# First scores from a quarter of each query block, the query rest of batch 0 in its own buffer, and the last highway pass in 128-column chunks

## The chip, the cores and the metric

The kernel runs on one core of one Trainium2 chip. The metric is the device time of one execution in microseconds (us), lower is better. Several runs are timed and their median is used; one execution more is recorded by the hardware profiler. The engines are called TensorE (PE in the profile, its weight loads PEld), VectorE (DVE), ScalarE (ACT), GpSimd (POOL) and SyncE (SP, which here only issues loads and stores).

## The reference: what is computed

Attention in which each query keeps only its 32 best keys, followed by a highway layer over the tokens:

```
q, k, v: 8 batches x 8 heads x 576 positions x 64, float32
scores = q @ k^T / 8
kth    = the 32nd largest score of each row
attn   = softmax of the scores >= kth, the others left out
y      = attn @ v                     # then heads side by side: x, 4608 x 512
H = relu(x @ w_h);  T = sigmoid(x @ w_t + b_t)
out = T * H + (1 - T) * x             # w_h, w_t: 512 x 512
```

## The kernel before

**Tiling.** The 576 positions of a batch are four chunks of 128 (J = 4) and a rest of 64 (R). Row `p` of the 128 partitions holds positions 4p to 4p+3, so query tile `qt` is made of the positions 4p + qt: one row in four. A *group* is one query tile of one batch; the rest rows of two batches together make a *joint* group. The order of the groups is that of the list `groups`; the very last one is called final and is `gl`, the one before it `gp`. A group of 128 rows has eight tiles, one for each head, taken two at a time: a *pair*, numbered n over the whole program, 0 to 143. The four pairs of group 0 use the heads 0-1, 2-3, 4-5, 6-7 and only the queries of row 0 in four, but all the keys.

**Loads and turning.** `load` (L105) brings two heads of q or k (`qin`, `kin`, 256 KB in two transfers) into SBUF; `load_rest` (L116) brings the 64 rest rows of all heads (`krest`, `qrest`, 128 KB each), `load_values` (L123) the values (1 MB) and their rest. TensorE turns each load into the layout that the scores need (`turn`, L138, four 128 x 128 transposes into one PSUM bank; `turn_rest`, L157), and ScalarE, or VectorE where `vec` is set, copies the bank into `kq`. The `kin` and `qin` pools have three buffers each, the rest tiles one. A bank for turning is one of two called `zt` or the only one called `fp`, which the highway layer uses too.

**One pair.** `scores` (L186) writes the scores of two tiles into the PSUM tile `ps`, of which there is one; `evac` (L206) has ScalarE copy it (with Relu) into a z buffer, `sc`; `tree` (L217) has VectorE take the larger of the left half, from `ps`, and the right half, from `sc`, into `hi`. So `ps` is free for the next scores only when both ScalarE and VectorE have read it. For each two pairs `folds` (L232) halves `hi` again, `minima` (L252) lets GpSimd work out the smaller halves, and `tops` and `rest` (L280, L301) find the 32nd largest with VectorE's eight-at-a-time maximum and replace. `mask` (L376) turns scores below the threshold into a penalty on ScalarE; `parts` (L425) transposes scores and penalty on TensorE and takes the exponential on ScalarE (`et`); `av` multiplies with the values and copies the result to `xs`, with the sum of the weights as a 65th column.

**The highway layer of a group.** `norm` (L490) divides by that sum; `ffn_x`, `ffn_h`, `ffn_r`, `ffn_d`, `ffn_t`, `ffn_e`, `ffn_o` (L588 to L685) turn x, make `h`, subtract half of x, make the tanh form of T, combine, and store. They are spread over the following steps.

**Order.** Every instruction on TensorE, VectorE, ScalarE and GpSimd keeps its written order (`Pinned`, L25), and so do the transfers issued through `ops.nc.queue`; other transfers on SP may be placed by the scheduler. Each engine runs its own list in order and waits at the head of it. A transfer on SP or ScalarE also waits until the transfer eight before it has landed, since there are eight semaphores for them. The loop at L892 takes one pair a step: tree of n, mask and values of earlier pairs, scores of n + 1, then the lists on VectorE. Before it, L832 to L856 load and turn the first data by hand. The loads of batch 1 begin at step 1 (`begin`, L802), and its turns use the `fp` bank at the end of steps from 4 on.

**The end.** From L979 the last three pairs (m, m + 1, m + 2) and the highway passes of `gp` and `gl` are written out by hand. There the final pass begins when both `values(m + 1)` and `values(m + 2)` are done: `norm(gl)`, `final_x(gl)`, then h, t, and the output in two halves. `judge_lists`, `judge_scales` and `judge` (L865 to L880) reduce range checks to one flag; if it is set, an exact and slower path follows (L1027), which these inputs do not take. All engines load the flag and branch on it at the end.

In the profile, instructions of the pinned engines all carry the line L35 of the `Pinned` helper, so they are told apart by the names of their tiles.

Of the kernel before, what the change touches and what calls it, by code (L numbers as in the profile page):

```python
# [8 lines left out]
AF = mybir.ActivationFunctionType  # L9
# [10 lines left out]
J = 4  # L20
# [47 lines left out]
class Ops:  # L68
# [36 lines left out]
    def load(self, pr, name, hp, eng=None, other=None):  # L105
# [4 lines left out]
        for hh in range(2):  # L110
            (other if other and hh else eng).dma_start(
                t[:, :, hh, :], src[hh].rearrange("(p j) d -> p j d", j=J)
            )
        pr[name, hp] = t

    def load_rest(self, pr, name, eng=None):  # L116
        t = self.ldpool.tile([self.R, self.H, self.D], FP32, tag=name, name=name, bufs=1)
        (eng or self.nc.sync).dma_start(
            t[:], pr[name[0]](0, self.H, J * self.P, self.S).rearrange("h p d -> p h d")
        )  # L120
        pr[name] = t
# [16 lines left out]
    def turn(self, pr, name, hp, bank=None, vec=False):  # L138
# [6 lines left out]
        for c in range(J):  # L145
# [5 lines left out]
        dst = pr["kq"][:, "kq".index(name[0]), hp, 0 : J * P]  # L151
        if vec:
            nc.vector.tensor_copy(dst, kqps[:])
        else:
            nc.scalar.copy(dst, kqps[:])

    def turn_rest(self, pr, h0, h1):  # L157
# [5 lines left out]
        for i, name in enumerate(("krest", "qrest")):  # L163
# [7 lines left out]
            pr["kq"][:, :, h0:h1, J * self.P : self.S], view[:, :, h0:h1, :]  # L171
        )

    def values_rest(self, pr):
        self.nc.scalar.copy(
            pr["vb"][0 : self.R, :, J, 0 : self.D], pr["vrest"][:]
# [40 lines left out]
    def tree(self, n):  # L217
# [3 lines left out]
        if n % 2 == 0:  # L221
# [5 lines left out]
        ps = self.st[n].pop("ps")  # L227
        nc.vector.tensor_tensor(
            hi[:, half, :], ps[:, :, 0:H1], self.st[n]["sc"][:, :, H1:S], ALU.max
# [271 lines left out]
    def norm_x(self, g):  # L501
# [8 lines left out]
        for hs in (slice(0, H // 2), slice(H // 2, H)) if g.final else (slice(0, H),):  # L510
            made = (nc.vector if g.final else nc.gpsimd).tensor_tensor(
                x3[:, hs, :],
                xs3[:, hs, 0:D],
                rinv[0:ql, hs].unsqueeze(2).to_broadcast([ql, hs.stop - hs.start, D]),
                ALU.mult,
            )
# [6 lines left out]
    def final_x(self, g):  # L523


        nc, P, n_g = self.nc, self.P, self.n_g
        g.xT = self.fpool.tile([P, n_g, P], BF16, tag="xT", name="xT")
        g.xh = self.fpool.tile([P, self.dm], FP32, tag="xh", name="xh")
        half = n_g // 2
        for i0 in (0, half):  # L530
            xtps = self.ztps.tile([P, 512], FP32, tag="zt", name="xtps")
# [569 lines left out]
```

## Time and profile before

| what | us |
|---|---|
| median of 3 runs (lowest to highest) | 874.24 (872.53 to 874.45) |
| the profiled execution, its own time | 874.66 |
| its span, first to last instruction | 872.9 |
| VectorE busy | 843.6 (97%) |
| first work of VectorE, a copy of turned queries | 7.22 |
| tree of pair 0, 1, 2, 3 starts | 10.56, 14.55, 19.02, 23.05 |
| last list operation of VectorE ends | 854.45 |
| last copy to `xs` ends | 861.18 |
| last output operation of VectorE ends | 868.23 |

The span is shorter than the execution's own time by what lies before the first and after the last instruction. Rows of a timeline give a start, a length, the engine, the tile written and the tiles read; what stands in brackets is how long the engine sat idle before it and what ended that. A wait is put down to the last thing that came. Granted clock is the share of full speed at which TensorE was allowed to run.

### The profile page before, as it was taken

The page shows a single profiled execution, that of the slowest core. Times are in us where ns is not written, and L with a number is a line of the kernel's source. Part 1 is how long each engine was busy: PE and PEld are TensorE (multiplying, and loading weights), DVE is VectorE, ACT ScalarE, POOL GpSimd, SP SyncE. Part 2 cuts the span into 40 slices and gives each one's busy share as a digit, 9 for nine tenths or more (in the row PEclk, how much of TensorE's full clock was granted, in tenths as well). Part 3 has the DMA queues.
Part 4 walks back from the last instruction along what each step waited for, and adds up shares of the span by engine and source line. Part 5 has one row for each costly group of instructions (what it writes and reads, how often), then busy time and mean ns, then how long its engine had stood idle before and what let it go on. Part 6 is the DMA issues. An engine that isn't in the chain of part 4 may idle for free.

```text
span 872.9 us, 19884 instructions
## 1 busy us (share of the span) xinstructions
PE 707.8 (81%) x6569; PEld 500.4 (57%) x6569; DVE 843.6 (97%) x4200; ACT 695.9 (80%) x1244; POOL 690.8 (79%) x447
## 2 busy tenths in 40 slices
PE   6777988879788788778788798887978878887975
PEld 5455655655565555655565565665556655555653
DVE  4999999999999999999999999999999999999995
ACT  3788878888788887888888887888878888677784
POOL 5788887888878888888888888878888888877880
PEclk9799999999999998999999999999989999899898
DMA  9553422234234331323323432323412111111111
GB/s 196 130 110 62 109 38 57 60 62 98 37 62 92 73 86 29 70 67 62 86 50 56 96 80 56 62 64 69 105 37 46 42 37 38 37 26 25 26 39 38
DMA packets 104494, 57.06 MB, mean 65 GB/s; under 512 B 82112, under 2 KB 91712, under 8 KB 104384
## 3 DMA queue, kind: packets, MB, share of 16 engines
q1 hardware_dynamic: 92768, 37.37, 17.0%
q0 software_dynamic: 10416, 17.96, 13.6%
q8 instruction: 53, 0.87, 0.4%
q14 instruction: 57, 0.47, 0.2%
q10 hardware_dynamic: 1200, 0.39, 0.2%
HBM read 30.67 MB, written 17.30 MB: 55 GB/s over the span
## 4 chain that ended last, share of the span: by engine, by line
DVE 90%; PE 4%; POOL 2%; DMA 1%; issue 1%; ACT 1%; SPq 0%; DVEq 0%; POOLq 0%; ACTq 0%
DVE w L35 48%; DVE m L35 18%; DVE hi L35 11%; DVE hh L35 6%; DVE h L35 4%; DVE d L35 3%; PE ps L35 1%; POOL hi L35 1%; PE zt L35 1%; POOL hh L35 1%; PE t L35 1%; DMA d<-xh 1%; DMA qrest<-in_q_dram 1%; PE zr L35 1%; ACT z L35 1%
## 5 line engine op out<-in xcount | busy, mean ns | idle before, releaser
L35 PE MATMUL ps<-kq 64*128 64x64 f32 (+3 forms) x1280 | 212.1, 457 | 89.5 <-DVE hi L35 85.4
L35 ACT ACTIVATE z<-ps 128x1152 f32<-128x1152 f32 x144 | 163.0, 1132 | 103.5 <-PE ps L35 101.2
L35 ACT ACTIVATE pen<-z,m 128x576 bf16<-128x576 f32 x288 | 225.9, 785 | 1.3 <-DVE m L35 1.1
L35 PE MATMUL zt<-ident,z 128*128 128x128 f32 x1152 | 225.7, 289 | 0.1
L35 PE MATMUL zt<-nident,pen 128*128 128x128 bf16 x1152 | 215.0, 225 | 0.3 <-ACT pen L35 0.3
L35 PEld LDWEIGHTS ps<-kq 64*128 64x128 f32 (+1 forms) x1280 | 107.5, 184 | 187.6 <-DVE hi L35 96.1
L35 POOL TENSOR_TENSOR hi<-z,hi 128x1152 int32<-128x1152 int32 x72 | 189.3, 2630 | 14.7 <-DVE m L35 9.2
L35 POOL TENSOR_TENSOR hh<-hi,hh 128x576 int32<-128x576 int32 x71 | 100.2, 1411 | 126.3 <-DVE w L35 126.3
L35 POOL TENSOR_TENSOR hi<-hi,z 128x1152 int32<-128x1152 int32 x72 | 190.3, 2643 | 5.7
L35 PEld LDWEIGHTS zt<-ident,z 128*128 128x128 f32 x1152 | 169.9, 147 | 19.1 <-ACT xT L35 0.6
L35 ACT ACTIVATE et<-zt 128x512 bf16<-128x512 f32 x288 | 161.5, 606 | 14.1 <-PE zt L35 13.3
L35 PEld LDWEIGHTS <-pen 128*128 128x128 bf16 x1440 | 160.0, 111 | 1.7 <-ACT pen L35 1.7
L35 DVE MAX8 m<-w 128x8 f32<-128x168 f32 x576 | 160.4, 320 | 0.0
L35 DVE MAX8 w<-hi 128x8 f32<-128x288 f32 x288 | 116.7, 447 | 0.0
L35 DVE TENSOR_TENSOR hi<-ps,z 128x576 f32<-128x576 f32 x144 | 106.8, 741 | 6.5 <-ACT z L35 6.5
L35 PE MATMUL zr<-v,et 128*128 128x65 bf16 (+1 forms) x1590 | 89.6, 196 | 18.5 <-ACT et L35 14.6
L35 POOL TENSOR_TENSOR hh<-hh,hi 128x576 int32<-128x576 int32 x71 | 100.0, 1408 | 5.6
L35 PEld LDWEIGHTS <-et 128*128 128x128 bf16 (+1 forms) x1600 | 69.8, 101 | 60.0 <-ACT et L35 46.0
L35 DVE MATCH_REPLACE8 w<-m,w 128x168 f32<-128x168 f32 x288 | 89.4, 318 | 0.0
L35 DVE MAX8 w<-hh 128x8 f32<-128x72 f32 x576 | 84.3, 221 | 0.0
L35 PE MATMUL zr<-ident,z 128*128 128x128 f32 x286 | 74.2, 313 | 3.5 <-ACT xs L35 3.5
L35 PE MATMUL zr<-nident,pen 128*128 128x128 bf16 x286 | 59.8, 230 | 0.3 <-ACT pen L35 0.3
(91 smaller groups left out, 1111.6 us busy)
## 6 DMA issues: line engine op xcount, KB each, us to landing
vin<-in_v_dram SPq DMA_DIRECT2D x8, 1024.0 KB, 5.6
kin<-in_k_dram SPq DMA_DIRECT2D x63, 128.0 KB, 3.4
qin<-in_q_dram SPq DMA_DIRECT2D x63, 128.0 KB, 3.1
out_dram<-x SPq DMA_DIRECT2D x30, 256.0 KB, 2.8
d<-xh POOLq DMA_DIRECT2D x30, 256.0 KB, 3.8
out_dram<-d POOLq DMA_DIRECT2D x30, 256.0 KB, 4.4
krest<-in_k_dram SPq DMA_DIRECT2D x8, 128.0 KB, 4.2
qrest<-in_q_dram SPq DMA_DIRECT2D x8, 128.0 KB, 5.0
```

Of the source, the lines that this page charges most:

```text
L35: return self._tc.keep_in_program_order(fn(*args, **kw))
```

## The change

Three things are changed, in loads, in the first steps and at the end.

**Loads and first scores.** `load` gets a first chunk `c0`: with `c0 = 1` it leaves out the first of the four query rows. `load_first` loads just that row, of some heads, into a new tile `qc` (one 256-byte piece in each 1 KB of the source), and `turn_first` turns it and has VectorE copy it. At the start, `kin` 0, two heads of `krest` (on ScalarE's queue) and two heads of `qc` are loaded first; then `kin` 1, the other heads of `qc` and of `krest`, `kin` 2 and 3. The transposes before the first scores are those of `kin` 0, one of `qc` and one of `krest`; the three extra warming transposes (`spin(3)`) go. `kin` 1 and the rest of `krest` are turned right after the first evacuation, `kin` 2 and `kin` 3 before scores 1 and 2.

**The query rest.** The remaining query rows of batch 0 (`qin`, three chunks) are loaded behind `kin` 3 and turned in steps 3 to 6, through the `fp` bank, and `qin` of the last two heads is loaded in step 4. `qrest` of batch 0 is loaded into the buffer of `qc` and turned in step 8; batch 1's `qrest` has its own buffer. In the emitted order SP issues batch 1's `qrest` ahead of `kin` 3.

**Trees of pairs 0 and 1.** They read both halves from the evacuated copy and none from `ps`.

**The last pass.** `final_x` is replaced. The 512 columns are handled as 256, 128 and 128: `final_norm` divides, `final_turn` transposes and copies, `final_h` and `final_t` add the chunk's products to sums left open in PSUM. The first 256 columns need only pairs up to m, and are taken before the values of pairs m + 1 and m + 2. The bias product opens the t sums rather than closing them. Part 1 of the last pair is moved ahead of `values(m + 1)`. The range check over the scales runs early, and a small one, `judge_last`, covers the last group. Most of the halved copy `xh` moves to GpSimd.

```diff
-    def load(self, pr, name, hp, eng=None, other=None):
+    def load(self, pr, name, hp, eng=None, other=None, c0=0):
...
             (other if other and hh else eng).dma_start(
-                t[:, :, hh, :], src[hh].rearrange("(p j) d -> p j d", j=J)
+                t[:, c0:J, hh, :],
+                src[hh].rearrange("(p j) d -> p j d", j=J)[:, c0:J, :],
             )
...
+    def load_first(self, pr, eng, h0, h1):
+        if not h0:
+            pr["qc"] = self.ldpool.tile(
+                [self.P, self.H, self.D], FP32, tag="qc", name="qc", bufs=1
+            )
+        src = pr["q"](h0, h1, 0, J * self.P)
+        eng.dma_start(
+            pr["qc"][:, h0:h1, :],
+            src.rearrange("h (p j) d -> p h j d", j=J)[:, :, 0, :],
+        )
+
+    def turn_first(self, pr, h0, h1):
+        nc, P = self.nc, self.P
+        kqps = self.ztps.tile([P, 512], FP32, tag="zt", name="kqps")
+        for hp in range(h0, h1):
+            nc.tensor.transpose(
+                kqps[:, hp * P : (hp + 1) * P],
+                pr["qc"][:, 2 * hp : 2 * hp + 2, :].rearrange("p h d -> p (h d)"),
+                self.ident[:],
+            )
+        nc.vector.tensor_copy(
+            pr["kq"][:, 1, h0:h1, 0:P],
+            kqps[:, h0 * P : h1 * P].rearrange("p (h q) -> p h q", q=P),
+        )
...
-        ps = self.st[n].pop("ps")
+        ps, sc = self.st[n].pop("ps"), self.st[n]["sc"]
+        if n < 2:
+            ps = sc
         nc.vector.tensor_tensor(
-            hi[:, half, :], ps[:, :, 0:H1], self.st[n]["sc"][:, :, H1:S], ALU.max
+            hi[:, half, :], ps[:, :, 0:H1], sc[:, :, H1:S], ALU.max
         )
...
+    def final_norm(self, g, i0, i1):
+        nc, P, D = self.nc, self.P, self.D
+        hs = slice(2 * i0, 2 * i1)
+        xs3 = g.xs[:].rearrange("p (h e) -> p h e", e=D + 1)
+        rinv = self.scales[:, g.gi, hs]
+        nc.vector.reciprocal(rinv, xs3[:, hs, D])
+        nc.vector.tensor_tensor(
+            g.x[:].rearrange("p (h d) -> p h d", d=D)[:, hs, :],
+            xs3[:, hs, 0:D],
+            rinv.unsqueeze(2).to_broadcast([P, 2 * (i1 - i0), D]),
+            ALU.mult,
+        )
+
+    def final_turn(self, g, i0, i1, xtps):
...
+        src = xtps[:, 0 : (i1 - i0) * P].rearrange("p (g j) -> p g j", j=P)
+        dst = g.xT[:, i0:i1, :]
+        cs = slice(i0 * P, i1 * P)
+        if i1 - i0 == 1 and i1 < self.n_g:
+            nc.scalar.mul(dst, src, 0.5)
+        else:
+            nc.vector.tensor_scalar_mul(dst, src, 0.5)
+        if i1 == self.n_g:
+            nc.scalar.mul(g.xh[:, cs], g.x[:, cs], -0.5)
+        else:
+            nc.gpsimd.tensor_scalar_mul(g.xh[:, cs], g.x[:, cs], -0.5)
...
-        for name in ("kin", "qin"):
-            ops.load(pr, name, 0, queue, nc.scalar)
-        for name in ("krest", "qrest"):
-            ops.load_rest(pr, name, queue)
-        for hp in (1, 2):
-            for name in ("kin", "qin"):
-                ops.load(pr, name, hp, queue)
+        ops.load(pr, "kin", 0, queue, nc.scalar)
+        ops.load_rest(pr, "krest", nc.scalar, 0, 2)
+        ops.load_first(pr, queue, 0, 2)
+        ops.load(pr, "kin", 1, queue)
+        ops.load_first(pr, queue, 2, H)
+        ops.load_rest(pr, "krest", queue, 2, H)
+        ops.load(pr, "kin", 2, queue)
...
         ops.turn(pr, "kin", 0, True)
-        spin(3)
-        ops.turn(pr, "qin", 0, True, True)
-        ops.turn_rest(pr, 0, 1)
-        for name in ("kin", "qin"):
-            ops.load(pr, name, 3, queue)
+        ops.turn_first(pr, 0, 1)
+        ops.turn_rest(pr, 0, 1, ("krest",))
+        ops.load(pr, "kin", 3, queue)
+        ops.load(pr, "qin", 0, queue, None, 1)
         ops.load_values(pr, queue)
+        ops.load(pr, "qin", 1, queue, None, 1)
+        ops.load(pr, "qin", 2, queue, None, 1)
         ops.scores(0, *pairs[0], preps[0])
         ops.evac(0)
+        ops.turn_first(pr, 1, NHP)
+        ops.load_rest(pr, "qrest", queue, tag="qc")
+        ops.turn(pr, "kin", 1, True)
+        ops.turn_rest(pr, 1, NHP, ("krest",))
...
-                if n + 1 < NHP:
-                    for name in ("kin", "qin"):
-                        ops.turn(
-                            pr, name, n + 1, True, n == 0 and name == "qin"
-                        )
-                    if n == 0:
-                        ops.turn_rest(pr, 1, NHP)
+                if n + 2 < NHP:
+                    ops.turn(pr, "kin", n + 2, True)
+                if NHP <= n + 1 < 2 * NHP:
+                    ops.turn(pr, "qin", n + 1 - NHP, None, 1)
+                if n == NHP:
+                    ops.load(pr, "qin", 3, None, None, 1)
+                if n == 2 * NHP:
+                    ops.turn_rest(pr, 0, NHP, ("qrest",))
...
+        ops.final_norm(gl, 0, 2)
+        ops.ffn_e(gp)
+        ops.ffn_o(gp, *out_rows(gp))
+        ops.final_turn(gl, 0, 2, banks[0])
         part, ends = ops.parts(m + 2, banks[3])
         part(0)
         ends()
-        ops.ffn_e(gp)
-        ops.ffn_o(gp, *out_rows(gp))
+        judge_lists()
+        judge_scales()
+        part(1)
         values(m + 1)
-        part(1)
-        judge_lists()
+        ops.final_norm(gl, 2, 3)
         values(m + 2)
-        ops.norm(gl)
-        ops.final_x(gl)
-        judge_scales()
-        ops.spare = [ops.fps.tile([P, 512], FP32, tag="fp", name="hps")]
-        ops.ffn_h(gl)
-        ops.ffn_r(gl)
+        ops.final_h(gl, 0, 2)
+        ops.final_turn(
+            gl, 2, 3, ops.ztps.tile([P, 512], FP32, tag="zt", name="xtps")
+        )
+        ops.final_norm(gl, 3, 4)
+        ops.final_t(gl, 0, 2)
+        ops.final_turn(
+            gl, 3, 4, ops.ztps.tile([P, 512], FP32, tag="zt", name="xtps")
+        )
+        ops.final_h(gl, 2, 3)
+        ops.final_t(gl, 2, 3)
+        judge_last(gl)
+        ops.final_h(gl, 3, 4)
         ops.ffn_d(gl)
+        ops.final_t(gl, 3, 4)
         judge()
-        ops.final_t(gl, banks[0:2])
         ops.final_o(gl, out_rows(gl), (nc.sync, ops.nc.scalar))
```

## The prediction

> **What bounds the kernel now.** I read the page first: busy shares, the forty slices, the chain that ended last.
>
> ```profile
> PE 707.8 (81%) x6569; PEld 500.4 (57%) x6569; DVE 843.6 (97%) x4200; ACT 695.9 (80%) x1244; POOL 690.8 (79%) x447
> ...
> DVE  4999999999999999999999999999999999999995
> ...
> DVE 90%; PE 4%; POOL 2%; DMA 1%; issue 1%; ACT 1%; SPq 0%; DVEq 0%; POOLq 0%; ACTq 0%
> ```
>
> VectorE is the bound: 843.6 of 872.9 us, and 90% of the chain. Only the first and last slice are not full, so what it loses, 29.3 us, lies at the two ends. Then I asked for VectorE's waits, in three windows: 0 to 40 us, 40 to 830, 830 to the end.
>
> ```profile
> DVE kq L35 <- PE kqps L35: 7.2, 1, 7.2
> DVE hi L35 <- ACT z L35: 6.1, 3, 2.6
> ...
> DVE hi L35 <- ACT z L35: 0.4, 1, 0.4
> ...
> DVE scales L35 <- ACT xs L35: 2.8, 1, 2.8
> DVE d L35 <- ACT t L35: 1.3, 2, 0.7
> ```
>
> 13.3 us are lost before 24 us, 0.4 us from 40 to 830, 5.5 us of waits in the tail (the smaller ones not shown); another 4.7 us pass behind VectorE's last operation. An edit in the body is worth nothing unless it makes VectorE wait; one at the ends is worth what it takes from these waits. The third view is the order of time, TensorE at the start; each row has its start, its length, and in brackets the wait before it:
>
> ```profile
> 6.34 0.84 PE L35 MATMUL kqps<-ident,qin 128*128 128x128 f32 x4 [0.36 <-DMA qin<-in_q_dram]
> 7.11 0.27 PE L35 MATMUL kqps<-ident,krest 64*128 64x64 f32 x1
> 7.91 0.27 PE L35 MATMUL kqps<-ident,qrest 64*128 64x64 f32 x1 [0.52 <-DMA qrest<-in_q_dram]
> 8.06 1.30 PE L35 MATMUL ps<-kq 64*128 64x512 f32 x8
> ...
> 10.20 0.63 PE L35 MATMUL kqps<-ident,qin 128*128 128x128 f32 x4 [0.26 <-DMA qin<-in_q_dram]
> ...
> 19.92 1.92 PE L35 MATMUL ps<-kq 64*128 64x512 f32 x8 [2.06 <-DVE w L35]
> ```
>
> The first scores wait for `qrest`, which group 0 does not use. The bracketed waits give a scale: 512 KiB (kin, qin) landed by 6.3 us, 768 KiB by 7.9, 1280 KiB by 10.2; kin alone, 256 KiB, by 4.26, where its transposes start.
>
> **The start.** The first scores now need kin 0 (256 KiB), two heads of krest (32) and two heads of one query row in four (64): 352 KiB, on the scale 5.0 us. Three spin transposes, three of the query and the one of qrest leave the path. Kin 0 is copied by ScalarE at 5.39 as before, in 0.58 us, to 5.97; the small query copy on VectorE (128 columns, about 0.25 us, scaled from 0.69 for 512) and the krest copy (0.27 or less) fit beside it. Scores 0 start at 6.0 instead of 8.06. Their 1.30 us is at full clock; the kin transposes at 4.26 (1.09 us for four) are still slow beside 0.66 at 9.29, so I add 0.4 us: end 7.7, evacuation (1.13) to 8.85.
>
> The second scores stand in TensorE's order behind the other three query transposes, kin 1, krest and now also kin 2. SP issues up to kin 2 eight loads at 0.65 us, to 6.0 us; they carry, with ScalarE's two, 256+32+64+256+192+96+256 = 1152 KiB: 9.6 us on the scale; four transposes take 0.66, to 10.25. The queries' rest (800 KiB) is there at 8.0, its transposes and kin 1's end at 9.15, ScalarE copies kin 1 (0.58) and krest (about 0.4) to 10.1. Scores 1 start at 10.3, not 12.06: they no longer wait for VectorE to read `ps`, since the first two trees read both halves from the evacuated copy (0.74 us from `ps`, 0.76 for the same shape from SBUF: nothing). Scores end 11.6, evacuation 12.75, tree 1 at 12.75 against 14.55: **1.8 us earlier**. VectorE's query copies (0.69 twice before; 0.25 and 0.55 now) lie in its idle time; the second stands ahead of tree 0, which then starts near 9.1, early enough.
>
> From tree 1 to tree 2 VectorE has 4.47 us of work (14.55 to 19.02), so tree 2 comes at 17.2. Scores 2 run at 12.75 to 14.05 and wait for nobody. Scores 3 still follow tree 2, whose `ps` they overwrite. TensorE thus idles 4 us instead of 2.06. Here a rule speaks against the change. The row: with 2.06 us idle, scores 3 took 1.92 us, the granted clock falling near their start (0.54 from 20 to 25 us); wholly slow ones took 2.4 (23.86 and 29.63). The Trainium skill, "TensorE: Matmul & The Clock Gate", section "What's actually happening", has the clock halved after an idle window of about 3.4 us, and windows that run freely. By the row the gain stays 1.8; by the rule scores 3 are slow throughout, 0.5 less. I take **1.5**, nearer the rule, since the idle time passes its window.
>
> The unknown is the loads. A second rule of the Trainium skill, "DMA: Bandwidth & Descriptors", section "Specifications", asks for 512 B or more per piece. The trace has 256 B pieces already in the kin and qin loads (17867 of 18893 packets of the first 30 us are under 512 B), so the scale contains that price; but their source runs are 1 KB, and the quarter loads' are 256 B. If these 256 KiB cost double, kin 2 counts as 1408 KiB: 10.7 us, and the gain falls by 1.1. In the other direction, with loads in time, ScalarE's copies set scores 1 near 9.6 and the gain is 2.4. Range of the start: 0.3 to 2.4.
>
> **The query rest in the body.** The queue now issues batch 1's qrest ahead of kin 3, which by the scale lands at 11.4 (1536 KiB) and is turned from 11.6, and then qin 0 without its first quarter, values, qin 1 and 2, and qrest in the freed buffer; qin 3 waits for a buffer behind batch 1's first loads. SP waits for the step 3 turn (about 20 us) before batch 1's qin 0; that load is needed at 39 us. Values take 1 MB; qin 1 behind them lands near 19 us and is needed at 25. No wait there. Steps 3 to 6 gain three transposes and a 384-column copy each (0.48 us on ScalarE), step 8 a 256-column one. In steps 5, 6 and 8 they use the one `fp` bank that a batch 1 turn has just filled, so TensorE waits for ScalarE's copy; behind it stand the `av` products, the next scores, and their evacuation. In the trace, evacuation 6 ends at 38.5 and tree 6 starts at 40.13; evacuation 7 ends 43.45, tree 7 starts 45.64. The turn adds some 1.1 us to each, accumulating: slack 1.6 becomes 0.5, 2.2 becomes 0.5, and by step 8 the slack (2.5 us) is back. Cost **0**; without that cover, up to 0.5 each.
>
> **The tail.** VectorE's list operations end at 854.45; then `d` of the group before and the judge reductions, 856.40 to 858.4, and:
>
> ```profile
> 861.21 0.20 DVE L35 RECIPROCAL scales<-xs 128x8 f32<-128x8 f32 x1 [2.82 <-ACT xs L35]
> 861.58 0.76 DVE L35 TENSOR_TENSOR x<-xs,scales 128x256 f32<-128x256 f32 x2 [0.17 <-DVE scales L35]
> 862.60 0.42 DVE L35 TENSOR_SCALAR xT<-xtps 128x256 bf16<-128x256 f32 x1 [0.26 <-PE xtps L35]
> ...
> 866.33 0.42 DVE L35 SCALAR_TENSOR_TENSOR d<-t,d 128x256 f32<-128x256 f32 x1 [0.63 <-ACT t L35]
> ```
>
> From 861.18, when the last `xs` is copied, 7.05 us run in series to 868.23. The change puts the first half of x (reciprocal 0.20, product 0.43, two transposes, `xT` 0.42) into the 2.82 us hole, and the hole also takes the scales' reduction. TensorE does part 1 of the last pair ahead of `values(m + 1)`: its end moves from 859.69 to 859.35, ScalarE evacuates it before both `xs` copies, and the last `xs` ends at 860.6 instead of 861.18 (0.6). Then the reciprocal and product for the last 128 columns (0.2 + 0.17 + 0.28) end at 861.4. The other chunks' products, six of 256 columns and two of 512, fill TensorE to 861.75 at full clock (1.3 us by 0.26 for 512 columns, 852.71); the last transpose 862.0, `xT` 0.25 to 862.3, the last h product 862.7, its two t products 862.95. On VectorE the last judge reductions (0.5) end at 862.9, `d` (0.6) at 863.5, the flag 1.05 us after `d` starts as before, at 864.0; both tanh are then done. The four output steps take 1.8 (866.33 to 868.23 less a wait of 0.1): last `o` at 865.8, not 868.23: 2.4. The flag comes only 1.7 earlier (865.70 before), and the branch that it releases on TensorE and GpSimd ended at about 870.0 before, 0.5 ahead of the last store: it may now end last, so I take **2.2**. Bounds: at half clock the products take 1.3 us more, leaving 1.0; with no such branch and every step back to back 2.9. The xh pieces on GpSimd (about 0.6 and 0.35 us, half and a quarter of its 1.3 for 512 columns) lie behind `o` of the group before, which ends at 857.9, and are done in time; the reciprocal and product that now stand ahead of that group's `d` delay it by 0.1, covered.
>
> Sum: 1.5 + 0 + 2.2 = **3.7 us**. The profiled execution is 874.66 (span 872.9, 1.8 around it): 871.0, span 869.2. Against the median of the runs, 874.24, which is 0.4 lower: **870.5 us**.
>
> **The rivals.** *One end only.* The loads come late, or scores 3 and the `fp` bank eat the start; or the half clock and the branch eat the tail. For it: TensorE's tail clock was 0.81 from 865 to 870 us. Against: either loss needs a late load or a half clock just there. 2.2 alone gives 872.0, 1.5 alone 872.7; with a stall of 1 us, 873.0.
> *Slower: the shared bank.* If TensorE stays at half clock past 45 us, steps 5, 6 and 8 each cost it 1.1 (scores 2.40 for 1.30), 1.2 (sixteen transposes 2.56 for 1.37) and 0.9 more for turns and `av`: 3.2, less 0.5 of slack, 2.7. Two such steps (5.4) undo the gain, 876.0; the third makes 878. It decides from 3.7 us of stall. Against it: the clock was back at 34.1 us, and a 6.8 us spell at half clock near 751 us cost VectorE 0.4.
> *No difference:* if GpSimd's minima set the pace of the body, an earlier start would be given back. GpSimd is 79% busy, holds 2% of the chain, and VectorE never waits on it here: 872.0 at best from the tail.
>
> **How the numbers follow.** Both ends 0.72 (868.9 to 872.4); one end 0.18; shared bank 0.06; given back 0.04. 0.2% is 1.75 us, about what a measurement here can tell from no change: faster means under 872.5. Both ends is nearly all faster (0.70), one end half (0.09), given back a little (0.01): 0.80; same 0.13; slower 0.07. The range goes to the one-end cases with a stall and to the better bounds: 868.6 to 873.2.
>
> **What would show it.** Right: scores 0 near 6.0 us, tree 1 near 12.7, tree 3 near 21.4; no wait of VectorE from 24 to 830 beyond 1 us; last `xs` near 857, last `o` near 862. Wrong: kin 2 landing after 10.7 us, waits of `hi` for `z` at 30 to 60 us, the last products at half clock.

## The result, and the profile after

| | before | after | change |
|---|---|---|---|
| median of the runs, us | 874.24 (872.53 to 874.45) | 870.98 (869.99 to 871.41) | ratio 0.9965 [0.9948, 0.9983] |
| the profiled execution, its own time | 874.66 | 870.94 | -3.7 |
| its span | 872.9 | 869.2 | -3.7 |
| trees of pairs 0, 1, 2, 3 start | 10.56, 14.55, 19.02, 23.05 | 9.18, 12.24, 16.71, 20.99 | tree 3 2.06 earlier |
| tree 3 to the end of the last list operation | 831.48 | 831.40 | -0.08 |
| last list operation to the last output operation (the tail) | 13.70 | 11.38 | -2.32 |
| last output operation to the end | 4.67 | 5.43 | +0.76 |

The last list operation is counted here to the end of its row, 854.53 before and 852.39 after. The 854.45 given ahead is the start of the operation that follows it; rows of one engine overlap a little. Spans are known to 0.1 us, so what lies behind the last output is good to about 0.05.

Measured a second time, beside the experiments, the changed kernel took 869.96 (0.9958 [0.9943, 0.9973]). It is faster by 3.3 to 4.1 us, and the last four rows of the table say where the profiled pair differs: 2.06 at the start, 2.32 in the tail, 0.08 between, and 0.76 given back behind the last output.

The page of the changed kernel, busy shares, slices and the chain that ended last:

```profile
PE 702.0 (81%) x6566; PEld 494.6 (57%) x6566; DVE 843.9 (97%) x4206; ACT 695.6 (80%) x1247; POOL 692.4 (80%) x449
...
DVE  4999999999999999999999999999999999999996
...
DVE 93%; PE 4%; ACT 1%; issue 1%; POOL 0%; DVEq 0%; ACTq 0%; POOLq 0%
```

VectorE does the same work (843.9 us against 843.6) in a shorter span; what went is idle time. Its waits, from 0 to 24 us, from 40 to 826, and from 826 to the end (us in total, times, longest):

```profile
DVE kq L35 <- PE kqps L35: 8.2, 2, 5.5
DVE hi L35 <- ACT z L35: 3.4, 2, 2.3
...
DVE hi L35 <- ACT z L35: 0.5, 1, 0.5
...
DVE xT L35 <- PE xtps L35: 0.7, 1, 0.7
DVE xT L35 <- PE t L35: 0.6, 1, 0.6
DVE d L35 <- ACT t L35: 0.3, 1, 0.3
DVE d L35 <- PE t L35: 0.2, 1, 0.2
DVE x L35 <- DVE scales L35: 0.2, 1, 0.2
```

The 2.8 us in which the first `scales` waited for the last `xs` are gone; what waits in the tail now is 2.0 us in five pieces. The body waits 0.5 us, as before. TensorE's start:

```profile
5.94 2.02 PE L35 MATMUL ps<-kq 64*128 64x512 f32 x8 [0.18 <-ACT kq L35]
...
9.73 1.30 PE L35 MATMUL ps<-kq 64*128 64x512 f32 x8
11.21 0.63 PE L35 MATMUL kqps<-ident,kin 128*128 128x128 f32 x4 [0.17 <-DMA kin<-in_k_dram]
12.26 1.30 PE L35 MATMUL ps<-kq 64*128 64x512 f32 x8 [0.42 <-ACT z L35]
17.51 2.27 PE L35 MATMUL ps<-kq 64*128 64x512 f32 x8 [3.96 <-DVE hi L35]
```

Scores 0 start 2.1 us earlier than before but take 2.02 us, because the full clock came only within them (1.30 us is the row at full clock, 2.40 at half). Scores 3 come after 3.96 us without work, and are slow again: the granted clock was halved from 17.69 to 31.34 us (before: from 20.44 to 34.10). VectorE's last rows:

```profile
861.13 0.69 DVE L35 SCALAR_TENSOR_TENSOR d<-hps,xh 128x512 f32<-128x512 f32 x1 [0.20 <-PE t L35]
861.74 0.27 DVE L35 TENSOR_REDUCE flag_f<-bps 1x1 f32<-1x128 f32 x1
862.05 0.14 DVE L35 CAST flag<-flag_f 1x1 int32<-1x1 f32 x1
862.12 0.40 DVE L35 SCALAR_TENSOR_TENSOR d<-t,d 128x256 f32<-128x256 f32 x1
...
863.35 0.42 DVE L35 TENSOR_TENSOR o<-x,d 128x256 f32<-128x256 f32 x1
```

The flag is out at 862.19, 1.6 us ahead of the last output at 863.77. At the flag all engines branch, and the program that follows is fetched by DMA. The DMA of the last 9 us, first before, then after:

```profile
out_dram<-o SPq DMA_DIRECT2D x1, 128.0 KB, 2.7
out_dram<-o ACTq DMA_DIRECT2D x1, 128.0 KB, 2.3
```

```profile
q8 instruction: 2, 0.03, 1.8%
q14 instruction: 6, 0.05, 1.8%
...
out_dram<-o SPq DMA_DIRECT2D x1, 128.0 KB, 3.7
out_dram<-o ACTq DMA_DIRECT2D x1, 128.0 KB, 3.4
```

The two stores take 1.0 and 1.1 us longer from issue to landing. Beside them two queues carry instructions, 0.08 MB; before, these were as many, but there the flag came 2.5 us ahead of the last output.

### The profile page after: what moved, and what is told of

It reads as the page before. It is cut to its first block, busy times and chain, and to the rows that moved or that the text cites. A ratio compares the mean times of both kernels' runs of the same rounds, so it can differ in the third digit from the quotient of the medians.

```text
span 869.2 us, 19896 instructions
## 1 busy us (share of the span) xinstructions
PE 702.0 (81%) x6566; PEld 494.6 (57%) x6566; DVE 843.9 (97%) x4206; ACT 695.6 (80%) x1247; POOL 692.4 (80%) x449
## 4 chain that ended last, share of the span: by engine, by line
DVE 93%; PE 4%; ACT 1%; issue 1%; POOL 0%; DVEq 0%; ACTq 0%; POOLq 0%
DVE w L35 50%; DVE m L35 19%; DVE hi L35 11%; DVE hh L35 6%; DVE h L35 4%; DVE d L35 3%; PE ps L35 1%; PE zt L35 1%; PE t L35 1%; ACT pen L35 0%; DVE scales L35 0%; ACT z L35 0%; ACT et L35 0%; PE warm L35 0%; PE kqps L35 0%
## 5 line engine op out<-in xcount | busy, mean ns | idle before, releaser
L35 PE MATMUL ps<-kq 64*128 64x64 f32 (+3 forms) x1280 | 215.9, 463 | 90.1 <-DVE hi L35 88.5
L35 PE MATMUL zt<-ident,z 128*128 128x128 f32 x1152 | 219.6, 284 | 0.0
L35 PE MATMUL zt<-nident,pen 128*128 128x128 bf16 x1152 | 209.6, 222 | 0.1
L35 PEld LDWEIGHTS zt<-ident,z 128*128 128x128 f32 x1152 | 166.2, 144 | 16.5
L35 PEld LDWEIGHTS <-pen 128*128 128x128 bf16 x1440 | 157.4, 109 | 2.2 <-ACT pen L35 2.0
L35 DVE TENSOR_TENSOR hi<-ps,z 128x576 f32<-128x576 f32 x142 | 104.9, 739 | 1.7 <-ACT z L35 1.6
L35 DVE MATCH_REPLACE8 w<-w,w 128x72 f32<-128x72 f32 x288 | 59.3, 217 | 0.0
```

What stands on the lines that cost most here:

```text
L35: return self._tc.keep_in_program_order(fn(*args, **kw))
```

## The experiments

The theory behind the first runs: the start and the tail each earn what their waits say, the body costs nothing because evacuations 6 and 7 end 0.4 and 0.5 us ahead of their trees, and the last 0.76 us are lost because the fetch that the flag sets off shares the DMA engines with the last stores. The rivals: one end alone does it; the body's cover is larger or smaller than read; the loss at the end is the branch itself. All are timed against the kernel before, whose medians beside the three sets of runs were 874.14, 873.99 and 874.07.

**The parts alone.** One kernel has only the new loads and first steps, the other only the new last pass.

```diff
 start_only
+        ops.load_first(pr, queue, 0, 2)          # and all other edits of the loads and steps 0 to 8
-        ops.final_norm(gl, 0, 2)                 # the last pass stays norm, final_x, ffn_h, final_t as before
```

> The changed loads, first scores, query rest and trees, with the last pass of before. Theory: the two ends are worth what the two profiles show, one by one: VectorE's last list operation comes 2.1 us earlier than before (852.3 instead of 854.45) and the tail is as long as before, so span 870.8, 2.1 us under before. Rival, that an earlier start only pays together with the new tail: less than 1 us under before. Rival, that the first part is worth the 1.5 us of the prediction and the tail 2.2: 1.5 under.

Measured: 873.82 (870.92 to 875.64), ratio 0.9995 [0.9981, 1.0008]; span 872.0. That is less than expected, and in its profile the reason is in TensorE's rows:

```profile
6.05 2.40 PE L35 MATMUL ps<-kq 64*128 64x512 f32 x8 [0.18 <-ACT kq L35]
8.38 0.90 PE L35 MATMUL kqps<-ident,qc 128*128 128x128 f32 x3
9.08 1.06 PE L35 MATMUL kqps<-ident,kin 128*128 128x128 f32 x4
10.06 0.58 PE L35 MATMUL kqps<-ident,krest 64*128 64x64 f32 x3
10.57 0.87 PE L35 MATMUL kqps<-ident,kin 128*128 128x128 f32 x4
11.38 1.30 PE L35 MATMUL ps<-kq 64*128 64x512 f32 x8
```

Here the full clock came at 11.06 us, not at 7.45 as in the changed kernel's profile, though both do the same until then. So all of TensorE's work from 6 to 11 us took its half-clock time, scores 1 started at 11.38 (9.73 there), tree 1 at 13.88 (12.24) and tree 3 at 22.77 (20.99): of the 2.06 us only 0.28 were left. The new start has TensorE's own work between scores 0 and scores 1 on its path, and so depends on when the clock comes.

```diff
 tail_only
-        ops.norm(gl)
-        ops.final_x(gl)
+        ops.final_norm(gl, 0, 2)                 # and all other edits behind the loop; the start stays as before
```

> The start of before with the chunked last pass. Theory: last list operation at 854.4 as before, last output operation 2.3 us earlier than before in relation to it (11.5 us after it instead of 13.8), but 0.7 of that lost again between the last output operation and the end (5.4 us instead of 4.65): 1.6 us under before, span 871.3. Rival, nothing lost behind the last operation: 2.3 under, span 870.6.

Measured: 871.59 (869.83 to 874.56), ratio 0.9974 [0.9962, 0.9987], so 2.5 us; its profiled execution was the slowest of its runs (874.56, span 872.8), with a tail of 14.78 us for 11.38. TensorE was at half clock until 857.08, 4.4 us past the last list operation. VectorE stood idle for 1.86 us behind its lists. The operation that comes next reads h of the group before, and TensorE's product for it lasted until 854.47 (1.89 us long, 1.04 in the changed kernel's profile); the profile puts the wait down to ScalarE's `pen`, which ended beside it at 854.37. The products for t behind it were as slow:

```profile
852.15 0.56 DVE L35 MAX8 m<-w 128x8 f32<-128x168 f32 x2
...
854.57 0.69 DVE L35 SCALAR_TENSOR_TENSOR d<-t,xh 128x512 f32<-128x512 f32 x1 [1.86 <-ACT pen L35]
854.83 1.90 PE L35 MATMUL t<-wt,xT 128*128 128x512 bf16 x4
```

In the changed kernel's profile, with the full clock back 1.9 us ahead of the end of the lists, the same operation of VectorE follows without a wait, and the same products take 1.02 us:

```profile
852.23 1.02 PE L35 MATMUL t<-wt,xT 128*128 128x512 bf16 x4
852.31 0.68 DVE L35 SCALAR_TENSOR_TENSOR d<-t,xh 128x512 f32<-128x512 f32 x1
```

Start 0.3 and tail 2.5 together are 2.8, less than the 3.3 to 4.1 of both; the intervals (start -0.7 to 1.7, tail 1.1 to 3.3) hold that. The tail by itself is shown to gain; the start by itself is not told from nothing by these runs.

**Where the flag is released.** Three kernels move it; nothing else differs from the changed kernel.

```diff
 flag_early
         ops.final_norm(gl, 3, 4)
+        judge_last(gl)
...
+        judge()
         ops.final_h(gl, 2, 3)
         ops.final_t(gl, 2, 3)
-        judge_last(gl)
...
-        judge()
 flag_late
-        judge()
         ops.final_o(gl, out_rows(gl), (nc.sync, ops.nc.scalar))
+        judge()
```

> The changed kernel with the check of the last group and the flag made earlier: judge_last ahead of the last transpose's copy, judge ahead of the last two chunks' products. In the changed kernel the flag is ready at 862.2, 0.9 us before the first of the last stores is issued (before: 1.5 us), and these stores land 3.7 and 3.4 us after their issue instead of 2.7 and 2.3. Theory, the flag's branch (its program fetch on the DMA engines, and its 3.7 to 4.2 us on TensorE) is in the stores' way: with the flag near 861.0 the last output operation ends near 863.4 (the flag no longer stands ahead of it on VectorE), the stores land in 2.3 to 2.7 us again, and the span is 868.1, 1.1 under the changed kernel. Rival, the stores are slow for another reason: only the 0.4 us on VectorE, span 868.8.

> The changed kernel with the flag made after the last output operation. Theory, the branch that waits for the flag ends last: the stores land in 2.3 to 2.7 us since nothing is fetched beside them, the last output operation ends near 863.4, but the flag comes near 863.8 and the branch ends some 4.5 us after it, so the span is 870.3, 1.1 over the changed kernel. Rival, the branch does not matter: 0.4 us under the changed kernel, span 868.8.

Measured: early 869.45 (868.93 to 870.87), 0.9951 [0.9933, 0.9970]; late 871.39 (870.73 to 873.45), 0.9977 [0.9966, 0.9988]; against the changed kernel's two medians 0.5 to 1.5 us faster and 0.4 to 1.4 slower. The intervals of the changed kernel (0.9943 to 0.9973, 0.9948 to 0.9983) overlap with both, so the runs alone do not tell it from either; early and late, timed side by side, are 1.9 us apart. The rest is read from the traces. The stores of the early and of the late one:

```profile
out_dram<-o SPq DMA_DIRECT2D x1, 128.0 KB, 2.1
out_dram<-o ACTq DMA_DIRECT2D x1, 128.0 KB, 2.2
```

```profile
out_dram<-o SPq DMA_DIRECT2D x1, 128.0 KB, 1.9
out_dram<-o ACTq DMA_DIRECT2D x1, 128.0 KB, 1.9
```

With the flag 2.8 us ahead of the last output, or behind it, the stores land in 1.9 to 2.2 us; with it 1.6 us ahead, in 3.3 to 3.7 in the changed kernel's two profiles. The stores are issued by the same code in all three. What differs is what runs beside them: while the stores' packets move, the changed kernel's trace has one instruction packet of 16 KB and four of 8 KB, the early one's two of 8 KB, the late one's none. So the stores' delay follows the fetch; which of its packets costs how much is not shown. But late, the branch itself ends last: TensorE's is over at 867.95, and 6.55 us pass from the last output to the end, against 5.43 and 4.75. Both mechanisms were real, each in its place. Of the three places the early one is best.

```diff
 flag_far
-        judge_last(gl)
...
+            vec.tensor_reduce(bad[:, 4:5], bad[:, 0:3], op=ALU.max, axis=AX.X)   # from the lists and scales alone
...
         ops.final_norm(gl, 2, 3)
         values(m + 2)
+        judge()
```

> The changed kernel with the flag made from the checks of the lists and of all other groups' scales before the last chunks; the last group's own scales are left out of the check. Theory, the branch is in the stores' way: with the flag near 859.5 the stores have the DMA engines for themselves, land in 2.3 to 2.7 us, last output operation near 863.3, span 868.0. Rival, the stores are slow for another reason: span 868.7 with 3.4 us or more to landing.

This kernel leaves out the check of the last group.

Measured: 870.84 (869.53 to 871.13), 0.9960 [0.9945, 0.9974]. The flag is out at 860.21, the stores land in 1.9 and 2.2 us and 4.92 us pass behind the last output, so nothing is gained over `flag_early` (860.14, 2.1 and 2.2, 4.75). Its tail was 12.89 us, with TensorE at half clock until 853.53, 1.9 us past the last list operation, and VectorE idle for 0.62 us behind it.

**TensorE's idle time ahead of scores 3.** Both kernels fill it at step 1, one with transposes of a constant, the other with products.

```diff
 spin_t
                 ops.scores(n + 1, g, pi, preps[g.b])
                 ops.evac(n + 1)
+                if n == 1:
+                    warm2 = ops.fps.tile([P, 512], FP32, tag="fp", name="warm2")
+                    for _ in range(26):
+                        ops.nc.tensor.transpose(warm2[:, 0:P], ident[:], ident[:])
 spin_m
+                    for _ in range(8):
+                        ops.nc.tensor.matmul(
+                            warm2[:], kq0[0:D, 1, 0, 0:P], kq0[0:D, 0, 0, 0:512]
+                        )
```

> The changed kernel with 26 idle transposes of the identity (0.13 us each, 3.4 us) on TensorE between scores 2 and scores 3, where it waits 3.96 us and then runs scores 3 in 2.27 us with the granted clock halved. Theory, the idle time halves the clock: scores 3 take 1.3 us, tree 3 starts when VectorE is free near 19.9 instead of 20.99, VectorE's wait there (1.10 us) goes, span 868.1. Rival, transposes do not hold the clock, or it falls for another reason: scores 3 stay at 1.9 to 2.4 us and the span at 869.2, or later if the transposes delay scores 3.

> As the one with idle transposes, but eight 64 x 512 float32 products (some 3.4 us) in the same place, into a bank that nobody reads. Theory, any work holds the clock: scores 3 in 1.3 us, span 868.1. Rival, only products hold it: this one gains 1.1 us and the transposes nothing. Rival, neither does: 869.2.

Measured: transposes 868.92 (868.55 to 872.63), 0.9950 [0.9930, 0.9969]; products 871.95 (870.65 to 873.03), 0.9973 [0.9963, 0.9984]. The first is 1.0 to 2.1 us under the changed kernel's two medians, with one run of six at 872.63; by these runs alone it is not told from the changed kernel. With the transposes:

```profile
13.56 3.06 PE L35 MATMUL warm<-ident 128*128 128x128 f32 x26
17.59 1.30 PE L35 MATMUL ps<-kq 64*128 64x512 f32 x8 [0.97 <-DVE hi L35]
...
21.00 1.30 PE L35 MATMUL ps<-kq 64*128 64x512 f32 x8 [1.64 <-DVE hi L35]
```

Scores 3 and 4 run at full clock, tree 3 no longer waits for its evacuation and starts at 20.09, 7.78 us behind tree 1 (8.75 in the changed kernel): 0.97 us, the price of the halved clock. The products kept the clock too, until 31.0 us, but they fill 16 records of 0.44 us, twice the time I had taken for them, and stood in front of scores 3:

```profile
14.83 6.65 PE L35 MATMUL warm<-kq 64*128 64x512 f32 x15
20.90 0.69 PE L35 MATMUL ps<-kq 64*128 64x512 f32 x1
```

Tree 3 came at 24.15. Its time says nothing of what the clock is worth: the filling was made too long.

**The turns in the body, doubled.** Each query turn of steps 3 to 6, and the rest's of step 8, is done twice, into the same place.

```diff
 turns_twice
-                    ops.turn(pr, "qin", n + 1 - NHP, None, 1)
+                    ops.turn(pr, "qin", n + 1 - NHP, None, 1, True)
+                    ops.turn(pr, "qin", n + 1 - NHP, None, 1)
```

> The changed kernel with each turn of the query rest (steps 3 to 6 and 8) done twice, the second time with the same result. In the changed kernel evacuations 6 and 7 end 0.4 and 0.5 us before VectorE wants them, 8 and 9 about 2 us. Theory, that the turns are hidden but have used up the cover: the second turn (1.1 us with its wait for the bank) makes VectorE wait about 0.7 us at tree 6 and 0.6 to 1.1 us at tree 7, nothing elsewhere, so 1.3 to 1.8 us over the changed kernel, span 870.5 to 871.0. Rival, the turns are far from VectorE's path: no wait of hi for z beyond 0.5 us, span 869.2.

Measured: 875.62 (874.07 to 878.38), 1.0024 [1.0012, 1.0037], 4.6 to 5.7 us slower than the changed kernel's two medians. VectorE's trees from 30 to 50 us, each with its wait for the evacuation:

```profile
33.65 0.76 DVE L35 TENSOR_TENSOR hi<-ps,z 128x576 f32<-128x576 f32 x1 [1.11 <-ACT z L35]
41.52 0.76 DVE L35 TENSOR_TENSOR hi<-ps,z 128x576 f32<-128x576 f32 x1 [2.00 <-ACT z L35]
48.06 0.76 DVE L35 TENSOR_TENSOR hi<-ps,z 128x576 f32<-128x576 f32 x1 [0.93 <-ACT z L35]
```

4.0 us of waits, more than twice what was expected, where the changed kernel has none in this stretch. The half clock lasted until 35.0 us here and until 31.34 in the changed kernel's first profile; but `start_only`, with single turns and half clock until 34.95, waited only 0.1 us at these trees, so it is the second turn that costs.

The single turns are free only just. The cover of 0.4 and 0.5 us is that of one profile; where the half clock lasts longer it is smaller. In `after_again` (until 32.64) evacuations 6 and 7 end 0.1 and 0.2 us ahead of their trees, and in `ps_trees` (until 33.71) VectorE waits 0.28 us for evacuation 6.

**The first two trees, and the start again.** The changed kernel itself, profiled and timed a second time, shows how far its start differs from execution to execution. Beside it, the one part of the start that was costed at nothing is undone.

```diff
 ps_trees
-        if n < 2:
-            ps = sc
```

> The changed kernel itself, profiled and timed again beside the others. Clock theory: the full clock comes at a moment that differs from execution to execution (7.45 us in the profile after; in traces of kernels with the same start it came between 4.3 and 11.1 us). Where it comes by 7.5 us, tree 1 starts at 12.0 to 12.5; where it comes after 10 us, at 13.7 to 13.9. So the runs should spread over 869.5 to 873, median 871.0 to 871.7. Rival, load theory: the start is paced by the landing of kin 2, then tree 1 follows that landing and not the clock.

> Undoes one part: the trees of pairs 0 and 1 read their left half from the scores' PSUM again. Scores 1 then wait for tree 0, scores 2 for tree 1 (0.74 us after its start, 13.0 for 12.26), and TensorE idles 3.2 us instead of 3.96 ahead of scores 3. If the part is worth nothing on the path: same as the changed kernel within 0.3 us (870.7 to 871.3), tree 2 unchanged. If the shorter idle time spares TensorE the halved clock: scores 3 in 1.3 instead of 2.27 us, tree 3 1 us earlier, 870.0. If scores 1 are held up by tree 0: 0.2 to 0.5 us slower, 871.4.

Measured: the changed kernel 869.96 (869.72 to 871.58); with trees 0 and 1 from PSUM 869.85 (869.32 to 873.38), 0.9953 [0.9936, 0.9969]. The trees' part is worth nothing: tree 1 12.16 and 12.17, tree 3 21.05 in both. TensorE idled 3.17 us for 3.96, and its clock was halved all the same, at 16.65 us. In the second profile of the changed kernel the clock came at 5.33 us, scores 0 took 1.30 us, and yet tree 1 started only 0.08 earlier than in the first:

```profile
5.95 1.30 PE L35 MATMUL ps<-kq 64*128 64x512 f32 x8 [0.27 <-ACT kq L35]
...
9.10 0.63 PE L35 MATMUL kqps<-ident,kin 128*128 128x128 f32 x4 [0.60 <-DMA kin<-in_k_dram]
9.65 1.30 PE L35 MATMUL ps<-kq 64*128 64x512 f32 x8
```

It waited for kin 2. So both theories of the start hold, one after the other: with the clock at 5.3 us the landing of kin 2 paces it, with the clock after 10 us TensorE's own work. The profiled run of `ps_trees`, 873.38, is 3.5 us over its median; that is its tail, 14.77 us against 11.10 in `after_again`, with half clock until 4.3 us past the end of the lists.

**The two gains together,** and with two warming transposes more ahead of scores 0:

```diff
 both_fixes: flag_early and spin_t in one kernel
 both_spin: the same, and
         ops.turn_first(pr, 0, 1)
+        spin(2)
         ops.turn_rest(pr, 0, 1, ("krest",))
```

> The flag released early together with 26 transposes that fill TensorE's idle time ahead of scores 3. If the two gains are independent: tree 3 near 20.1 instead of 21.0 (0.9 us), last output to the end 4.75 instead of 5.43 (0.7 us): span 867.6 from the profile after, less what else the two runs gained; time 868.4 to 869.3. Rival, the two gains were the same run to run chance: no better than either alone, 869.4 or more.

> The same, with two warming transposes back between the transposes of the first queries and those of the krest heads, so that TensorE has no idle time ahead of scores 0. They cost the path 0.2 us with the full clock and 0.4 with half. If idle time ahead of scores 0 decides when the full clock comes: it comes by 7.6 us in the profile, tree 1 by 12.6, and the runs spread less at the slow end than without them; median 868.5 to 869.5. If it does not decide: 0.2 to 0.4 us slower than without, the same spread.

Measured: 868.74 (868.17 to 869.34), 0.9943 [0.9925, 0.9962]; with the two transposes 868.48 (867.64 to 870.14), 0.9936 [0.9918, 0.9955]. Both are 1.2 to 1.5 us under the changed kernel beside which they ran (869.96), with the slowest run of `both_fixes` under the changed kernel's fastest, and 5.3 to 5.6 under the kernel before; `both_fixes` has its tree 3 at 19.78 and 4.69 us behind its last output, as expected of independent gains. Between the two there is no difference that these runs can tell. In the profile of the second the clock came at 6.18 and tree 1 at 12.29; whether the two transposes bring it sooner stays open, since it came by 7.5 us in nine of the eleven profiles with the new start and without them.

**All profiles beside each other.** Times in us. "Clock up" is when the full clock came at the start (the trace's first record of it, which the lengths of TensorE's rows bear out); "clock back" is when it last returned from half, counted from the end of the last list operation (minus: before it); "idle" is VectorE's wait right behind that operation, and a part of the tail; the tail and the rest are as in the first table. `before` and `start_only` have the old last pass, `before` and `tail_only` the old start.

| kernel | clock up | tree 1 | tree 3 | clock back | idle | tail | last output to end |
|---|---|---|---|---|---|---|---|
| before | 6.79 | 14.55 | 23.05 | -28.54, half again from 863.54 | 0 | 13.70 | 4.67 |
| start_only | 11.06 | 13.88 | 22.77 | -6.55 | 0 | 12.59 | 5.53 |
| tail_only | 7.16 | 14.28 | 22.14 | +4.37 | 1.86 | 14.78 | 5.31 |
| after | 7.45 | 12.24 | 20.99 | -1.85 | 0 | 11.38 | 5.43 |
| after_again | 5.33 | 12.16 | 21.05 | -6.74 | 0 | 11.10 | 5.25 |
| ps_trees | 6.41 | 12.17 | 21.05 | +4.31 | 1.91 | 14.77 | 4.81 |
| turns_twice | 4.29 | 12.45 | 21.15 | -1.91 | 0 | 11.36 | 5.52 |
| spin_t | 4.29 | 12.31 | 20.09 | -28.17 | 0 | 10.91 | 4.83 |
| spin_m | 10.52 | 13.68 | 24.15 | -28.58 | 0 | 10.90 | 5.42 |
| flag_far | 7.03 | 12.08 | 20.97 | +1.94 | 0.62 | 12.89 | 4.92 |
| flag_early | 5.81 | 12.13 | 21.02 | -6.47 | 0 | 10.99 | 4.75 |
| flag_late | 5.50 | 11.98 | 20.86 | -6.54 | 0 | 10.93 | 6.55 |
| both_fixes | 4.97 | 12.00 | 19.78 | -6.17 | 0 | 10.89 | 4.69 |
| both_spin | 6.18 | 12.29 | 20.07 | +1.88 | 0.61 | 12.82 | 4.68 |

Two columns order the others. With the new start, tree 1 comes at 11.98 to 12.45 wherever the clock was up by 7.45 us (ten profiles), and at 13.68 and 13.88 in the two where it came after 10. With the new last pass, the tail is 10.89 to 11.10 us where the clock was full from 6 us before the end of the lists on, about 11.4 where it returned 1.9 before, 12.8 to 12.9 where 1.9 after, and 14.8 where 4.3 to 4.4 after. From the shortest to the longest these are 3.9 us, about what the whole change is worth. Each row is one execution; how often a kernel meets which clock is not shown.

## Why the prediction was right, and where it was not

The time was right: 870.5 forecast, 870.98 and then 869.96 measured, and the profiled pair differs by 3.7 us as the sum said. Of its terms the body was right, the start and the tail were off by +0.6 and -0.6. That they cancelled is luck: the two errors, in the landing of a load and in a row measured at half clock, have nothing to do with each other.

**The start, 1.5 forecast, 2.06 in the profile.** Scores 0 came as worked out (6.0; 5.94), their end too (7.7; 7.96), with the slow clock named. The step that was mis-sized is "9.6 us on the scale" for kin 2: its two halves landed at 8.2 and 8.7. So scores 1 came at 9.73, not 10.3, and tree 1 at 12.24, not 12.75: this half microsecond is nearly the whole difference. The scale was right for the loads of before (there 1024 KiB had landed at 8.9 and 1280 at 10.1); the new ones, 1152 KiB with the quarter loads among them, landed sooner (8.7, where 1152 KiB of before had landed at 9.5). So the price that the worst case put on the 256 B runs, after the rule on pieces under 512 B, does not show here. In the second profile TensorE waited for kin 2 until 9.1, still ahead of the forecast. From tree 1 to tree 3 the forecast had 8.65 us, the profile 8.75: here the weighing of the clock rule was right, scores 3 slow throughout (2.27 us), and `spin_t` gives its price, 0.97 us.

What the forecast did not have is that the start now leans on the moment at which the clock comes. It assumed 0.4 us for it; the profiles have 0 to about 1.6 us. With a late clock the gain of the start is 0.3 us, the lower bound of its range, by another cause than the loads named there.

**The body, 0 forecast, 0.08 gained in the profiled pair.** Slack of 0.5 and 0.5 was forecast for evacuations 6 and 7, 0.4 and 0.5 were found, and VectorE waited 0.5 us from 40 to 826, 0.4 before. Other profiles have less slack, down to a wait of 0.28 in `ps_trees`, so the cost is 0 to 0.3 us and goes with the clock. `turns_twice` shows that this was near: the rival of the shared bank is a mechanism of this kernel, and one more turn a step brings the slower time. The forecast let it decide from 3.7 us of stall; with 4.0 us the doubled kernel ended at 1.0024. The reading that all of VectorE's lost 29.3 us lie at the two ends was too wide: from 24 to 830 us it was busy for 800.59 of 806.00, so 5.4 us went in the body, nearly all in short gaps, and they are there after the change too (796.64 of 802.00 from 24 to 826).

**The tail, 2.4 less 0.2 forecast, 2.32 less 0.76 in the profile.** The 2.32 look like the 2.4, but for the wrong reason in part. The step that failed is "7.05 us run in series": that row of before was measured with TensorE at half clock, from 863.54 to 866.95, which the rivals' paragraph mentions (0.81) and the sum does not use. The same code in `start_only`, at full clock, took 5.77 us from the last `xs` (860.70) to the last output (866.47). TensorE's last pass in before and in `start_only`:

```profile
863.08 1.48 PE L35 MATMUL hps<-wh,xT 128*128 128x512 bf16 x4 [0.18 <-DVE xT L35]
...
864.56 1.06 PE L35 MATMUL t<-wt,xT 128*128 128x256 bf16 x4
```

```profile
862.61 1.04 PE L35 MATMUL hps<-wh,xT 128*128 128x512 bf16 x4 [0.18 <-DVE xT L35]
...
863.59 0.60 PE L35 MATMUL t<-wt,xT 128*128 128x256 bf16 x4
```

At equal clock the pair is `start_only` and `after_again` (clock back 6.5 and 6.7 us ahead): tail 12.59 and 11.10, 1.5 us. Of these, 0.55 are the earlier last `xs` (6.82 and 6.27 us behind the lists; 0.6 was forecast) and 0.94 the shorter series (5.77 and 4.83; 1.8 was forecast).

The 0.2 for the branch was 0.76 in the profiled pair, and again the pair misleads: the old last pass in `start_only`, with its flag 1.7 us ahead of the last output, lost 5.53 us behind it, more than the new one. In before, the slow clock had spread flag and output to 2.5 us, and its stores landed in 2.7 and 2.3. So the fetch under the stores is not a cost of the change alone; with a flag 1.6 to 1.7 us ahead of the last output it is there in the old and in the new last pass, and `flag_early` shows that some of it can be had back. The forecast named the branch as what may end last; in the changed kernel the two end almost together, TensorE's branch at 867.06 (4.2 us long; 3.4 in `flag_early`) and the last store at 867.2.

Tail and end together, at equal clock: 12.59 + 5.53 = 18.12 against 11.10 + 5.25 = 16.35, 1.8 us, where 2.2 were forecast. `tail_only`, timed, says 2.5 with an interval of 1.1 to 3.3.

**The landmarks.** "Last xs near 857, last o near 862" did not follow from the forecast's own sum: 860.6 and 865.8 less 1.5 are 859.1 and 864.3. Measured were 858.96 and 863.77. The others hold: tree 3 near 21.4 (20.99), no wait above 1 us in the body, kin 2 well before 10.7.

**The rivals.** "One end only" gave 872.0 to 873.0; the timed start alone is no gain that its runs can tell from nothing (873.82) and the tail alone is 871.59, yet with both the kernel is 1.6 us under the tail alone (869.96 against 871.59, not timed side by side). What the start earns with an early clock is shown by the traces; what it earns on average is not settled better than by the interval. "Given back by GpSimd" did not happen: the body took 831.40 us against 831.48.

## What to carry to other kernels

Before you sum up a gain from a row of the old profile, look at which clock that row was measured with; a difference of one profiled pair at an end of a kernel can be half clock. An end is best compared between two profiles in which the clock stood alike there. Let the flag that ends a kernel be known so early that most of the fetch behind its branch is over when the last stores go out. And an edit that takes waits for loads off the start puts the engine's own speed on the path in their place: look there next.

## What the runs showed of the hardware

- The clock changes on a grid of 3.41 us in every trace, and the grid lies differently in each execution: 17.69 to 31.34 in the changed kernel is four such steps, 7.45 to 17.69 three. The Trainium skill, "TensorE: Matmul & The Clock Gate", section "What's actually happening", has the windows run freely; the traces agree, and show the size of it here: up to 1.9 us at tree 1 (11.98 to 13.88), 3.9 us in the tail. Why two of the profiles had the clock one window later than others with nearly the same grid (a step of the grid lies at 7.65 in `start_only`, at 7.45 in the changed kernel) is open.
- No wholly idle window was needed to lose the clock: 2.06 us of idle time (before), 3.17 (`ps_trees`) and 3.96 ended in it. In before, the window of the grid that ended in the fall, 17.03 to 20.44, held those 2.06 us and 1.35 us of work. With 0.97 us, in `spin_t`, it was kept.
- The same page's section "Part 4: PE-mode transpose" says that transposes do not bring the full clock. Here those of float32 did: in `spin_t` and `turns_twice` it came at 4.29 us, when TensorE had run nothing in this execution but transposes, from 1.6 us on. In `spin_t`, the four transposes of kin 0 behind the first twelve took 0.67 us, where 1.06 to 1.09 is the row at half clock (the changed kernel, `start_only`):

```profile
1.58 2.82 PE L35 MATMUL warm<-ident 128*128 128x128 f32 x12 [1.58 <-POOL ident masks.py:199]
4.19 0.67 PE L35 MATMUL kqps<-ident,kin 128*128 128x128 f32 x4
```

  And 26 of them kept it, in `spin_t`, `both_fixes` and `both_spin`: scores 3 in 1.30 us in all three, against 2.22 to 2.40 in the kernels with the new start and no filling. That this wasn't the fewer microseconds of idle time alone, no run separates.
- Two stores of 128 KB land in 1.9 to 2.2 us with the flag 2.8 us or more ahead of the last output, or behind it; in 2.3 and 2.7 with it 2.5 ahead (before), and in 2.7 to 4.0 with it 1.6 to 1.7 ahead, when the program behind the branch is fetched at the same time.
